# Three value buffers, reciprocals on SyncE's queue and an earlier normalization in an attention kernel with two feed-forward layers

## The chip, the core and the metric

The kernel runs on one core of a Trainium2 chip. Its engines work side by side: TensorE (PE; its weight loads are shown as PEld), VectorE (DVE), ScalarE (ACT), GpSimd (POOL) and SyncE (SP), which here does nothing but issue DMA transfers. Each engine takes its own instructions in order and waits where an operand or a buffer isn't ready. The 16 DMA engines of the core are shared by all transfers, whichever engine issued them. The metric is the time of one execution in microseconds, the median over several.

## The reference

Attention with a soft cap on its scores, then a feed-forward layer, then a gated one with a root-mean-square norm in front of it. All of it is float32.

```python
scores = scale * np.matmul(q, k.transpose(0, 1, 3, 2))     # q, k, v: (2, 12, 448, 64)
scores = cap * np.tanh(scores / cap)
attn = np.exp(scores - np.max(scores, axis=-1, keepdims=True))
attn = attn / (np.sum(attn, axis=-1, keepdims=True) + 1e-09)
x = np.matmul(attn, v)                                     # turned to (896, 768)
h = x @ w_in                                               # (768, 2048)
x = (h * (1.0 / (1.0 + np.exp(-1.702 * h)))) @ w_out       # (2048, 768)
xn = x / np.sqrt(np.mean(x * x, axis=-1, keepdims=True) + 1e-06) * rms_g
g = xn @ w_gate                                            # (768, 1536), w_val alike
out = (g * (1.0 / (1.0 + np.exp(-g))) * (xn @ w_val)) @ w_out2
```

## The kernel before

The 24 heads are taken two at a time: 12 pairs, six of each batch. A loop (in `attention`) runs over steps 0 to 12. Step p makes the scores of pair p, and in the same step finishes the pair before it. So that every product keeps nearly all float32 bits, operands are split into a rounded high part and a remainder, and three products are summed.

What one step does, engine by engine:

- **PE**: the score products of the pair in four chunks of keys (`scores`, three chunks of 128, and `scores_last`), the transposes of the pair two ahead (`turn`), the first chunk of the next pair, the weighted values of the pair before (`outputs(p - 1)`, line 360, 16 products), and the sums of its weights (`sums(p - 1)`, line 392). Outputs, sums and last chunks share two PSUM buffers (`ps_v`). So `outputs` has to wait until the buffer of the sums of one step before has been read by the reciprocal.
- **ACT**: tanh and exp of every chunk (lines 344 and 345).
- **DVE**: splits the turned q and k of the pair two ahead (lines 295 and 296), adds the first two chunks of weights (`add_two`, line 376) and for the first six pairs the third too (`add_third`, line 379), copies the outputs out of PSUM (`z`, line 368), normalizes an older pair (`normal`: lines 422, 434 and 441), and takes the reciprocal of the sums (`rs`, line 397). Where `add_third` isn't done, PE sums the third chunk by four products of its own (`v<-tt,ones`).
- **POOL**: a small copy of k (`kb`), and the two transfers that spread the reciprocals. `keep_recips` writes four rows of 224 reciprocals to DRAM (`recs<-rs`), and a step later `spread` reads them back as two rows of 448, each repeated on 64 partitions (`r<-recs`, 128 x 448 floats). The product with `r` (line 422) needs it. Pairs 9, 10 and 11 don't use this way: `spread_product` spreads their reciprocals by PE.
- **SP**: loads of q and k (`load_k`, `load_q`, eight transfers for a group of one or two pairs, into two buffers `raws`), of v (`load_v`, one transfer `vn` and two `ve`, into two buffers taken by the group's number modulo 2), and of the feed-forward weights (`load_to`, 768 KB each, `raw`). The groups are (first pair, pairs): (0,1), (1,2), (3,1), (4,2), (6,2), (8,2), (10,2).

The order on every engine is the order of the calls in this loop; no scheduler moves anything. A normalization comes four pairs late: step p calls `normal(p - 4)` behind `outputs(p - 1)`. Weight loads follow at the end of steps 1, 2 and 4, value loads at the end of steps 1, 3, 4, 6 and 8. The pair-by-pair decoding of the first weight units stands in two tables by step, `plan_a` for ACT and `plan_d` for DVE: a weight arrives as 64-bit words and is turned into a high and a low part (`size`, `clip`, `field`, `top`, `low`, `high_part`, `low_part`). `low` of a unit also issues the load of the unit three later.

Step 12 has no scores: it finishes pair 11 and goes over into `rest`, where PE multiplies by the feed-forward weights (lines 619 to 621, later 829) until the end. Its first two columns of work need the weight units 0 and 1 decoded and the first six pairs normalized; between them stands the `spread_product` of pair 11.

Of the kernel before, what the change touches and what calls it, by code (L numbers as in the profile page):

```python
# [18 lines left out]
def attn_moe_kernel(  # L19
# [174 lines left out]
    def attention():  # L194
        with ExitStack() as actx:
# [15 lines left out]
            vns = [ap_.tile([128, 4, NC, D], F32, name=f"vn{i}", bufs=1) for i in range(2)]  # L211
            ves = [ap_.tile([128, 2, 2, D], F32, name=f"ve{i}", bufs=1) for i in range(2)]
# [36 lines left out]
            def load_v(g):  # L249
# [3 lines left out]
                    out=vns[g % 2][:, 0:2 * n].rearrange("p h c d -> p h (c d)"),  # L253
                    in_=v[b, h0:h0 + 2 * n, 0:NC * 128].rearrange("h (p c) d -> p h (c d)", c=NC),
                )
                for e in range(2):
                    nc.sync.dma_start(
                        out=ves[g % 2][half[e], 0:n, e], in_=rows(v, p0, n, NC * 128, S)[:, e:2 * n:2]
                    )
# [91 lines left out]
            def outputs(p, cs=range(NC + 1)):  # L351
# [5 lines left out]
                for c in cs:  # L357
                    for e in range(2):
                        w = vns[g % 2][:, 2 * i + e, c] if c < NC else ves[g % 2][:, i, e]
# [12 lines left out]
            SH = S // 2  # L372

# [7 lines left out]
            def sums(p):  # L381

                ps = ps_v.tile([128, 512], F32, tag="v", name="v")
                for c in (1, NC) if p < NP else (1, 2, NC):
# [14 lines left out]
            def keep_recips(p):  # L399
                rs = nr[p]  # L400
                nr[p] = dram.tile([4, SH], F32, tag="recs", name="recs", bufs=3)
                nc.gpsimd.dma_start(out=nr[p], in_=rs[0:128:32])

            def spread(p):
                d = nr[p].rearrange("(e j) n -> e (j n)", j=2)
                nr[p] = zrp.tile([128, S], F32, tag="r", name="r", bufs=3)
                nc.gpsimd.dma_start(out=nr[p], in_=d.unsqueeze(1).to_broadcast([2, 64, S]))
# [58 lines left out]
            def warm_up(times):  # L466
# [6 lines left out]
                5: [(size, 0)], 7: [(size, 1)], 9: [(high_part, 0)], 11: [(high_part, 1)],  # L473
                12: [(square, 2), (sign, 2), (mask, 2), (square, 3), (sign, 3), (mask, 3)],
# [3 lines left out]
                10: [(top, 1), (low, 1), (low_part, 0)], 11: [(low_part, 1)],  # L478
# [16 lines left out]
            for p in range(NPR + 1):  # L495
                if p < NPR:
# [14 lines left out]
                    if p + 2 < NPR:  # L511
                        turn(p + 2)
                        split_kq(p + 2)
                    if 0 < p < NPR - 1:
                        s0 = scores(p + 1, 0)
# [4 lines left out]
                else:  # L520
                    decode(plan_a, p)
                if p == 0:
# [5 lines left out]
                if p >= 4:  # L528
                    normal(p - 4)
# [13 lines left out]
                if p < NP:  # L543
# [7 lines left out]
                decode(plan_d, p)  # L551

                for g, at_ in ((2, 0), (3, 0), (4, 1), (5, 3), (6, 5)):
                    if p == at_:
                        load_k(g)
                        load_q(g)
                if p in (1, 3, 4, 6, 8):
                    load_v(2 + (1, 3, 4, 6, 8).index(p))
                if p in (1, 2, 4):
                    load_to((1, 2, 4).index(p))  # L560
# [374 lines left out]
```

## Time and profile before

| What | us |
|---|---|
| Time, median of 3 runs | 610.75 (607.37 to 612.85) |
| The profiled execution | 607.63 |
| Its span, first to last instruction | 605.9 |
| PE busy in the span | 596.1 (98%) |
| DVE busy | 456.7 (75%) |
| ACT busy | 395.0 (65%) |
| POOL busy | 69.2 (11%) |

PE is called busy nearly always, but its products are pipelined and their ends are modelled, so short waits hide in that number. A wait is better read from the times at which the same piece of work starts in two steps that follow each other. Attention takes the first 106.6 us or so; there PE, ACT and DVE all have about the same amount of work in a step, and the feed-forward part behind it is PE alone.

### The profile page before, as it was taken

What the parts mean: (1) busy time and instruction counts of PE and PEld (TensorE: products, weight loads), DVE (VectorE), ACT (ScalarE), POOL (GpSimd) and SP (SyncE); (2) the same over time, 40 slices, a digit from 0 to 9 for tenths busy, and PEclk for the clock granted to TensorE, in tenths of its full rate; (3) what the DMA queues carried; (4) which work ended last, traced back from release to release, by engine and by line L of the source; (5) the groups of instructions that cost most, each with busy time, mean ns of one, the idle gap of its engine ahead of it and who ended that gap; (6) DMA issues with size and microseconds to landing.
All of it is one profiled execution on the core that took longest, in us unless ns stands there. A gap on an engine that the chain in (4) does not pass through costs nothing.

```text
span 605.9 us, 8623 instructions
## 1 busy us (share of the span) xinstructions
PE 596.1 (98%) x3405; PEld 505.9 (83%) x3405; DVE 456.7 (75%) x558; ACT 395.0 (65%) x529; POOL 69.2 (11%) x95
## 2 busy tenths in 40 slices
PE   8999999999999999999999999999999999999997
PEld 5454554889988899888888888899989999999997
DVE  3988998698774636667788899994588897688842
ACT  6998998499775547777676666674555493366400
POOL 4221321000000000000022203200022200122100
PEclk9999999999999999999999999999999999999999
DMA  6777232064343332333333333433233342232012
GB/s 152 157 194 187 67 113 84 9 203 151 111 157 104 105 105 80 123 111 105 104 105 109 100 106 107 140 117 106 62 124 116 116 134 85 96 104 105 0 79 105
DMA packets 78568, 67.18 MB, mean 111 GB/s; under 512 B 29440, under 2 KB 75830, under 8 KB 78528
## 3 DMA queue, kind: packets, MB, share of 16 engines
q1 hardware_dynamic: 74064, 64.27, 33.9%
q0 software_dynamic: 3664, 2.16, 1.3%
q8 instruction: 27, 0.44, 0.3%
q10 hardware_dynamic: 800, 0.20, 0.1%
q14 instruction: 13, 0.11, 0.1%
HBM read 63.80 MB, written 2.78 MB: 110 GB/s over the span
## 4 chain that ended last, share of the span: by engine, by line
PE 88%; DMA 7%; ACT 3%; DVE 1%; issue 1%; POOL 0%; POOLq 0%
PE b L621 22%; PE b L620 22%; PE b L619 22%; PE b L829 14%; DMA recs<-rs 4%; PE v L360 3%; PE s L322 2%; DMA ve<-in_v 1%; DMA r<-recs 1%; ACT tt L345 1%; ACT tt L344 1%; PE v L392 1%; PE v L468 1%; PE v L332 1%; PE t L274 0%
## 5 line engine op out<-in xcount | busy, mean ns | idle before, releaser
L621 PE MATMUL b<-x,ring 128*128 128x512 f32 (+1 forms) x480 | 174.3, 363 | 0.0
L620 PE MATMUL b<-x,ring 128*128 128x512 f32 (+1 forms) x480 | 174.1, 363 | 0.0
L619 PE MATMUL b<-x,ring 128*128 128x512 f32 (+1 forms) x480 | 173.9, 362 | 0.0
L619 PEld LDWEIGHTS b<-x,ring 128*128 128x128 f32 x480 | 90.1, 188 | 10.4 <-issue 0.3
L620 PEld LDWEIGHTS b<-x,ring 128*128 128x128 f32 x480 | 90.1, 188 | 9.9
L621 PEld LDWEIGHTS b<-x,ring 128*128 128x128 f32 x480 | 90.1, 188 | 9.4
L829 PE MATMUL b<-ring,uA 128*128 128x384 f32 x504 | 87.8, 334 | 0.0
L829 PEld LDWEIGHTS b<-ring,uA 128*128 128x128 f32 x504 | 87.4, 188 | 0.0
L154 DVE SCALAR_TENSOR_TENSOR dec<-raw,dec 128x768 uint32<-128x768 uint32 x66 | 67.8, 1027 | 24.7 <-ACT dec L150 23.4
L160 DVE SCALAR_TENSOR_TENSOR dec<-raw,dec 128x768 uint32<-128x768 uint32 x68 | 73.1, 1075 | 1.1
L175 ACT ACTIVATE ring<-dec 128x768 fp32r<-128x768 f32 x68 | 56.7, 834 | 21.9 <-DVE dec L166 13.7
L180 DVE TENSOR_TENSOR ring<-dec,ring 128x768 fp32r<-128x768 f32 x68 | 66.8, 983 | 4.5 <-ACT ring L175 4.5
L621 PE MATMUL b<-g,ring 128*128 128x384 f32 (+1 forms) x192 | 70.0, 365 | 0.0
L620 PE MATMUL b<-g,ring 128*128 128x384 f32 (+1 forms) x192 | 69.9, 364 | 0.0
L619 PE MATMUL b<-g,ring 128*128 128x384 f32 (+1 forms) x192 | 69.6, 362 | 0.0
L166 DVE SCALAR_TENSOR_TENSOR dec<-raw,dec 128x768 uint32<-128x768 uint32 x68 | 64.9, 954 | 1.5
L146 ACT ACTIVATE dec<-dec,edge 128x768 f32<-128x768 f32 x66 | 61.5, 932 | 1.0
L142 ACT ACTIVATE dec<-raw 128x768 f32<-128x768 f32 x66 | 59.2, 897 | 0.5 <-DVE ring L180 0.5
L150 ACT ACTIVATE dec<-dec 128x768 f32<-128x768 f32 x66 | 55.6, 843 | 1.5
L797 POOL TENSOR_TENSOR a<-a,gg 128x512 f32<-128x512 f32 (+1 forms) x18 | 29.6, 1646 | 188.6 <-DVE gg L790 188.6
L800 ACT ACTIVATE uA<-a 128x512 fp32r<-128x512 f32 (+1 forms) x24 | 13.9, 578 | 46.3 <-POOL a L797 34.5
L651 DVE TENSOR_TENSOR g<-gg,g 128x384 fp32r<-128x384 f32 (+1 forms) x32 | 20.0, 625 | 25.9 <-ACT g L648 25.7
(107 smaller groups left out, 680.2 us busy)
## 6 DMA issues: line engine op xcount, KB each, us to landing
raw<-in_moe_w_out SPq DMA_DIRECT2D x20, 768.0 KB, 4.2
raw<-in_moe_w_in SPq DMA_DIRECT2D x16, 768.0 KB, 4.5
raw<-in_moe_w_gate SPq DMA_DIRECT2D x12, 768.0 KB, 4.2
raw<-in_moe_w_val SPq DMA_DIRECT2D x12, 768.0 KB, 4.2
raw<-in_moe_w_out SPq DMA_DIRECT2D x8, 512.0 KB, 3.6
out<-oacc SPq DMA_DIRECT2D x6, 384.0 KB, 2.3
raw<-in_moe_w_out SPq DMA_DIRECT2D x8, 256.0 KB, 3.1
r<-recs POOLq DMA_DIRECT2D x9, 224.0 KB, 7.4
```

Source lines behind the costliest of these rows:

```text
L142: nc.scalar.activation(out=f(d), in_=f(hi), func=AF.Square, scale=2.0 ** 15)
L146: nc.scalar.activation(out=f(d), in_=f(d), func=AF.Sign, bias=edge)
L150: nc.scalar.activation(out=f(d), in_=f(d), func=AF.Relu, scale=2.0 - 2.0 ** -23)
L154: nc.vector.scalar_tensor_tensor(out=d, in0=hi, scalar=3, in1=d, op0=ALU.logical_shift_left, op1=ALU.bitwise_and)
L160: nc.vector.scalar_tensor_tensor(out=d, in0=hi, scalar=0xC0000000, in1=d, op0=ALU.bitwise_and, op1=ALU.bitwise_or)
L166: nc.vector.scalar_tensor_tensor(out=d, in0=lo, scalar=29, in1=d, op0=ALU.logical_shift_right, op1=ALU.bitwise_or)
L175: nc.scalar.activation(out=t[:, 0], in_=f(dec_t[w][0]), func=AF.Copy)
L180: nc.vector.tensor_tensor(out=t[:, 1], in0=f(d), in1=f(t[:, 0]), op=ALU.subtract)
L619: nc.tensor.matmul(out=wide(o, b), lhsT=w0, rhs=x0, start=first, stop=False)
L620: nc.tensor.matmul(out=wide(o, b), lhsT=w0, rhs=x1, start=False, stop=False)
L621: nc.tensor.matmul(out=wide(o, b), lhsT=w1, rhs=x0, start=False, stop=last)
L829: nc.tensor.matmul(out=os_[t][n][:, 0:HW], lhsT=uA[xi][:, i, tok], rhs=w[:, wi, n * HW:(n + 1) * HW], start=(i == 0 and xi == 0 and wi == ...
```

## The change

Five things are changed, all in `attention`:

1. The value buffers `vns` and `ves` are three each, taken by the group's number modulo 3.
2. `keep_recips` and `spread` issue their transfers on SP's queue, not on POOL's.
3. `normal` is called for pair p - 3 in steps 3 to 11 (before: pair p - 4 in steps 4 to 12). The calls for the pairs 9 and 10 stay where they were.
4. `add_third` is also done for pairs 10 and 11, and `sums` leaves the third chunk out for them.
5. `high_part` of units 0 and 1 is done in steps 10 and 12 (before 9 and 11), `low_part` in steps 11 and 12 (before 10 and 11), ahead of the sums of pair 11 in step 12. The loads of q, k, v and weights are called in the middle of a step, ahead of `spread` and `keep_recips`. Values are loaded in steps 1, 2, 4, 5 and 7, and the first three weight units in steps 2, 4 and 6.

```diff
-            vns = [ap_.tile([128, 4, NC, D], F32, name=f"vn{i}", bufs=1) for i in range(2)]
-            ves = [ap_.tile([128, 2, 2, D], F32, name=f"ve{i}", bufs=1) for i in range(2)]
+            vns = [ap_.tile([128, 4, NC, D], F32, name=f"vn{i}", bufs=1) for i in range(3)]
+            ves = [ap_.tile([128, 2, 2, D], F32, name=f"ve{i}", bufs=1) for i in range(3)]
...
+            THIRD = {*range(NP), NPR - 2, NPR - 1}
...
-                for c in (1, NC) if p < NP else (1, 2, NC):
+                for c in (1, NC) if p in THIRD else (1, 2, NC):
...
-                nc.gpsimd.dma_start(out=nr[p], in_=rs[0:128:32])
+                nc.sync.dma_start(out=nr[p], in_=rs[0:128:32])
...
-                nc.gpsimd.dma_start(out=nr[p], in_=d.unsqueeze(1).to_broadcast([2, 64, S]))
+                nc.sync.dma_start(out=nr[p], in_=d.unsqueeze(1).to_broadcast([2, 64, S]))
...
+                    for g, at_ in ((2, 0), (3, 0), (4, 1), (5, 3), (6, 5)):
+                        if p == at_:
+                            load_k(g)
+                            load_q(g)
+                    if p in (1, 2, 4, 5, 7):
+                        load_v(2 + (1, 2, 4, 5, 7).index(p))
+                    if p in (2, 4, 6):
+                        load_to((2, 4, 6).index(p))
                     if 0 < p < NPR - 1:
                         s0 = scores(p + 1, 0)
...
                 else:
                     decode(plan_a, p)
+                    decode(plan_d, p)
...
-                if p >= 4:
-                    normal(p - 4)
+                if 3 <= p < NPR:
+                    normal(p - 3)
...
-                if p < NP:
+                if p in THIRD:
                     add_third(p)
...
-                decode(plan_d, p)
-
-                for g, at_ in ((2, 0), (3, 0), (4, 1), (5, 3), (6, 5)):
...
-                if p in (1, 3, 4, 6, 8):
-                    load_v(2 + (1, 3, 4, 6, 8).index(p))
-                if p in (1, 2, 4):
-                    load_to((1, 2, 4).index(p))
+                if p < NPR:
+                    decode(plan_d, p)
```

On SP's queue, behind the value load of step 1, the order was this (two lines of the kernel move to other numbers with the change: 402 becomes 403, 407 becomes 408):

```order
L252 DMA vn_104<-in_v 128x2x192
L257 DMA ve_106<-in_v 64x64 x2
L113 DMA raw<-in_moe_w_in 128x6x256 x2
L237 DMA kq_103<-in_k 64x4x64
L239 DMA kq_103<-in_k 128x4x64 x3
L245 DMA kq_103<-in_q 64x4x64
L245 DMA kq_103<-in_q 128x4x64 x3
L252 DMA vn_105<-in_v 128x4x192
L257 DMA ve_107<-in_v 64x2x64 x2
```

And with the change, from the reciprocals that step 1 keeps on to those that step 3 keeps:

```order
L403 DMA recs<-rs 4x224
L252 DMA vn_104<-in_v 128x4x192
L257 DMA ve_107<-in_v 64x2x64 x2
L113 DMA raw<-in_moe_w_in 128x6x256
L408 DMA r<-recs 128x1x448
L403 DMA recs<-rs 4x224
L237 DMA kq_103<-in_k 64x4x64
L239 DMA kq_103<-in_k 128x4x64 x3
L245 DMA kq_103<-in_q 64x4x64
L245 DMA kq_103<-in_q 128x4x64 x3
L408 DMA r<-recs 128x1x448
L403 DMA recs<-rs 4x224
```

The value load that stood behind a weight pair and eight loads of q and k now stands ahead of them, and each `r` stands behind all loads of its step.

On DVE, from the reciprocal of pair 9's sums (step 10) into step 12, before:

```order
L397 RECIPROCAL rs<-v 128x224
L160 SCALAR_TENSOR_TENSOR dec<-raw,dec 128x768
L166 SCALAR_TENSOR_TENSOR dec<-raw,dec 128x768
L180 TENSOR_TENSOR ring<-dec,ring 128x768
L376 TENSOR_TENSOR ts<-tt 128x896
L368 COPY z<-v 128x448
```

and with the change:

```order
L398 RECIPROCAL rs<-v 128x224
L380 TENSOR_TENSOR ts<-ts,tt 128x896
L160 SCALAR_TENSOR_TENSOR dec<-raw,dec 128x768
L166 SCALAR_TENSOR_TENSOR dec<-raw,dec 128x768
L377 TENSOR_TENSOR ts<-tt 128x896
L368 COPY z<-v 128x448
```

The addition of the third chunk came in, and the low part of unit 0 (line 180) went out, to a place behind the normalizations of step 11, where both low parts now stand in a row ahead of the last reciprocal:

```order
L398 RECIPROCAL rs<-v 128x224
L380 TENSOR_TENSOR ts<-ts,tt 128x896
L426 TENSOR_TENSOR z<-z,late 128x448
L435 CAST x_66<-z 128x448
L442 TENSOR_TENSOR x_67<-z,x_66 128x448
L180 TENSOR_TENSOR ring<-dec,ring 128x768 x2
L398 RECIPROCAL rs<-v 128x224
```

Before, a whole normalization (lines 422, 434 and 441) stood between the low part of unit 1 and that last reciprocal; it is now done in step 11.

## Rows read from the trace of the kernel before

**Rows 1.** Busy time of the two stages; stretch, length, then each engine's busy us:

```profile
0.00:106.60 106.60, 101.03 (x873) 52.82 (x873) 87.26 (x107) 94.88 (x110) 27.94 (x67) 1.00 0.52 136
106.60:605.90 499.30, 495.07 (x2536) 453.06 (x2532) 369.48 (x451) 300.16 (x420) 41.29 (x28) 1.00 0.32 106
```

**Rows 2.** TensorE in order of time, outputs of pairs 3 to 6 (start us, us):

```profile
41.00 2.48 PE L360 MATMUL v<-tt,vn 128*64 128x448 f32 x12
...
44.16 0.59 PE L392 MATMUL v<-ts,ones 128*32 128x224 f32 x8
...
48.52 2.48 PE L360 MATMUL v<-tt,vn 128*64 128x448 f32 x12
...
52.64 0.97 PE L360 MATMUL v<-tl,ve 128*64 128x448 f32 x2 [0.90 <-DMA ve<-in_v]
...
57.90 2.48 PE L360 MATMUL v<-tt,vn 128*64 128x448 f32 x12
...
65.42 2.48 PE L360 MATMUL v<-tt,vn 128*64 128x448 f32 x12
```

**Rows 3.** VectorE in order of time, steps 3, 6 and 10:

```profile
36.78 0.63 DVE L368 COPY z<-v 128x448 f32<-128x448 f32 x1 [0.57 <-PE v L360]
37.67 1.56 DVE L397 RECIPROCAL rs<-v 128x224 f32<-128x224 f32 x1 [0.26 <-PE v L392]
...
61.94 0.61 DVE L422 TENSOR_TENSOR z<-z,r 128x448 f32<-128x448 f32 x1
...
63.56 1.55 DVE L397 RECIPROCAL rs<-v 128x224 f32<-128x224 f32 x1
...
92.41 0.62 DVE L368 COPY z<-v 128x448 f32<-128x448 f32 x1 [1.93 <-PE v L360]
```

**Rows 4.** GpSimd in order of time, the issue of one `r`:

```profile
69.17 0.80 POOL L407 DMA_DIRECT2D r<-recs  x1 [5.02 <-DMA recs<-rs]
```

**Rows 5.** Line 407, and the nearest load by SP: issue to landing, us:

```profile
DMA to landing us min/median/max: 6.8/7.4/11.9
...
vn<-in_v SPq DMA_DIRECT2D x2, 192.0 KB, 2.8
```

**Rows 6.** DMA in four stretches; the last two numbers are share of 16 engines and GB/s:

```profile
31.50:34.50 3.00, 3.00 (x30) 1.82 (x31) 2.59 (x4) 2.97 (x4) 0.57 (x1) 1.00 1.05 367
58.50:59.50 1.00, 1.00 (x8) 0.34 (x6) 0.96 (x2) 1.00 (x2) 0.00 (x0) 1.00 0.83 205
62.00:62.50 0.50, 0.50 (x9) 0.47 (x8) 0.50 (x2) 0.50 (x1) 0.50 (x2) 1.00 1.01 318
95.00:99.00 4.00, 3.69 (x21) 1.52 (x19) 3.97 (x5) 2.57 (x4) 0.00 (x0) 1.00 0.13 49
```

**Rows 7.** SyncE's issues in order of time, steps 1 and 2:

```profile
27.41 1.13 SPq L257 DMA_DIRECT2D ve<-in_v  x2
28.59 1.18 SPq L113 DMA_DIRECT2D raw<-in_moe_w_in  x2
```

**Rows 8.** VectorE and TensorE where attention ends, in order of time:

```profile
104.90 0.95 DVE L180 TENSOR_TENSOR ring<-dec,ring 128x768 fp32r<-128x768 f32 x1
107.45 0.63 DVE L422 TENSOR_TENSOR z<-z,r 128x448 f32<-128x448 f32 x1 [1.60 <-DMA r<-recs]
...
109.09 1.55 DVE L397 RECIPROCAL rs<-v 128x224 f32<-128x224 f32 x1
...
106.63 0.44 PE L619 MATMUL b<-x,ring 128*128 128x384 f32 x1
...
109.68 0.34 PE L621 MATMUL b<-x,ring 128*128 128x384 f32 x1
...
111.33 0.44 PE L619 MATMUL b<-x,ring 128*128 128x384 f32 x1
```

**Rows 9.** Third chunk, groups by line (busy us, mean ns): added on DVE, summed on PE:

```profile
L379 DVE TENSOR_TENSOR ts<-ts,tt 128x896 f32<-128x896 f32 x6 | 6.3, 1048 | 0.1
...
L392 PE MATMUL v<-tt,ones 128*32 128x224 f32 x48 | 3.4, 353 | 0.0
```

More of the change, by code (lines that the diff above doesn't have):

```diff
@@ L252, in load_v @@
                 nc.sync.dma_start(
-                    out=vns[g % 2][:, 0:2 * n].rearrange("p h c d -> p h (c d)"),
+                    out=vns[g % 3][:, 0:2 * n].rearrange("p h c d -> p h (c d)"),
                     in_=v[b, h0:h0 + 2 * n, 0:NC * 128].rearrange("h (p c) d -> p h (c d)", c=NC),
@@ L257, in load_v @@
                     nc.sync.dma_start(
-                        out=ves[g % 2][half[e], 0:n, e], in_=rows(v, p0, n, NC * 128, S)[:, e:2 * n:2]
+                        out=ves[g % 3][half[e], 0:n, e], in_=rows(v, p0, n, NC * 128, S)[:, e:2 * n:2]
                     )
@@ L358, in outputs @@
                     for e in range(2):
-                        w = vns[g % 2][:, 2 * i + e, c] if c < NC else ves[g % 2][:, i, e]
+                        w = vns[g % 3][:, 2 * i + e, c] if c < NC else ves[g % 3][:, i, e]
                         nc.tensor.matmul(
@@ L472, in attention @@
             plan_a = {
-                5: [(size, 0)], 7: [(size, 1)], 9: [(high_part, 0)], 11: [(high_part, 1)],
-                12: [(square, 2), (sign, 2), (mask, 2), (square, 3), (sign, 3), (mask, 3)],
+                5: [(size, 0)], 7: [(size, 1)], 10: [(high_part, 0)],
+                12: [(high_part, 1), (square, 2), (sign, 2), (mask, 2), (square, 3), (sign, 3), (mask, 3)],
             }
@@ L477, in attention @@
                 6: [(clip, 0), (field, 0)], 7: [(top, 0)], 8: [(low, 0)], 9: [(clip, 1), (field, 1)],
-                10: [(top, 1), (low, 1), (low_part, 0)], 11: [(low_part, 1)],
+                10: [(top, 1), (low, 1)], 11: [(low_part, 0)], 12: [(low_part, 1)],
             }
@@ L550, in attention @@
                     normal(p - 2)
-                decode(plan_d, p)
-                for g, at_ in ((2, 0), (3, 0), (4, 1), (5, 3), (6, 5)):
-                    if p == at_:
-                        load_k(g)
-                        load_q(g)
-                if p in (1, 3, 4, 6, 8):
-                    load_v(2 + (1, 3, 4, 6, 8).index(p))
-                if p in (1, 2, 4):
-                    load_to((1, 2, 4).index(p))
+                if p < NPR:
+                    decode(plan_d, p)
             return spread_product, norm_mul, norm_hi, norm_lo
```

## Prediction

> **What bounds the kernel now.** I read the stages first. From 106.6 us on PE is busy for 495.07 of 499.30 us [rows 1]; the change touches nothing there, so that part can only start earlier or later. All that can be won or lost lies ahead of 106.6 us. There PE is busy for 101.03 and DVE for 87.26 of 106.60 us, so neither is idle for long, and what a single wait is worth must be read from times of start.
>
> On PE the outputs of one pair start 7.52 us after those of the pair before (41.00 to 48.52), but the next start 9.38 later (48.52 to 57.90): in between stands a wait for `ve`, shown as 0.90 us, and the difference of 1.86 us is its price [rows 2]. On DVE a step from one normalization to its reciprocal takes 1.62 us (61.94 to 63.56) and a reciprocal 1.56 [rows 3]. Behind attention's end a last `r` is late: DVE waits for it for 1.60 us and then normalizes until 109.09, ahead of the last reciprocal, for which PE's second column of feed-forward work waits; that column starts at 111.33, 4.70 us after the first [rows 8].
>
> Then the transfers of the reciprocals. `r` takes 6.8 us at the least from issue to landing, where an SP load of nearly its size (192 KB) takes 2.8 [rows 5]. The reason stands in a stretch in which `r` alone is in flight: 0.13 of 16 engines are busy, that is two, and they move 49 GB/s [rows 6]. The 224 KB (229 kB) of one `r` take 229/49 = 4.7 us, and 2.1 us lie around that. I put 1.5 of them ahead of the data and 0.6 behind, which is an estimate. Two engines fit the source, which is two rows, each repeated for 64 partitions.
>
> **What each part costs.**
>
> *Third value buffer, values loaded sooner.* The load that came late goes to SP at about 29 us (behind the value load of step 1, 28.54 below) and is needed behind 48.52. This gives back the 1.86 us on PE [rows 2]. Weight units are loaded up to two steps later and are decoded from step 5 on, the last of the three only in step 12, so that costs nothing; were a unit not there, ACT would stop at its first decoding.
>
> *Reciprocals through SP.* The pattern of `r` isn't changed, only the queue. No row shows such a pattern on SP's queue. Its bounds are the 2.8 us of the SP load and the 6.8 us of `r` itself [rows 5]; I take 6.8, 4.7 of it on two engines, since the two rows of the source are what makes the difference and they stay. The Trainium skill, "DMA: Bandwidth & Descriptors", section "Why a DMA increments its semaphore by 16 and not by 1", says that the number of engines is the largest up to 16 that divides the slowest dimension of both sides, for transfers from POOL and from SP alike. The trace agrees for POOL's queue (0.13 of 16 [rows 6]), and no run here shows it for SP's. By that rule it is two here as well, and the sum is the one below; were it POOL's alone, it would be that of the first rival.
>
> What the queue does change is the order. SP's transfers go through these two engines one behind the other, and each `r` now stands behind the loads of its step. Their time on the engines comes from full-rate stretches [rows 6]: a weight unit (786 kB at 367 GB/s) 2.1 us, a group's q and k (918 kB at 205) 4.5, a group's values (459 kB at 318) 1.4. SP now also waits for each step's reciprocal before it goes on to the next step's loads; these are needed two steps later or more, so that wait costs nothing by itself. POOL loses its waits for `recs` (5.02 us in one step [rows 4]), but only the small `kb` copies stand behind them and nobody waits for those.
>
> *Normalization a pair sooner.* `r` of pair p - 3 is needed in step p, one step earlier than before. What is late then is DVE: behind its wait stand the reciprocal of the step, and behind that PE's next outputs, which need the reciprocal's PSUM buffer. So I follow `r` from pair to pair. With every `r`, normalization (1.62), reciprocal (1.56) and outputs follow; the next `r` is due 3.16 us of outputs (41.00 to 44.16 [rows 2]) and 0.68 for the hand-over and the copy (0.63 [rows 3]) later, 3.84 in all.
>
> - r(0): SP is through with the value load of step 1 at 28.54 (27.41 + 1.13 [rows 7]). Then come `recs`, three value transfers and a weight unit, 0.6 us an issue [rows 7], so `r` is issued at 31.6. The weight unit, issued at 31.0, has its data on the engines from 32.5 to 34.6. r(0) lands at 34.6 + 4.7 + 0.6 = 39.9. It is due behind the copy at 36.78, at 37.3 [rows 3]: 2.6 late. Reciprocal until 43.1, outputs of pair 3 at 43.1 and not 41.00.
> - r(1) stands behind eight loads of q and k: 39.3 + 4.5 + 4.7 + 0.6 = 49.1. Due at 43.1 + 3.84 = 46.9: 2.2 late. Outputs of pair 4 at 52.3.
> - r(2) stands behind values and a weight unit: 48.5 + 1.4 + 2.1 + 4.7 + 0.6 = 57.3. Due at 56.1: 1.2 late. Outputs of pair 5 at 60.5.
> - r(3) stands behind q, k and values: 56.7 + 4.5 + 1.4 + 4.7 + 0.6 = 67.9. Due at 64.3: 3.6 late. Outputs of pair 6 at 71.1, where they were at 65.42 [rows 2]: 5.7 us later.
> - r(4) stands behind a weight unit: 67.3 + 2.1 + 4.7 + 0.6 = 74.7. Due at 74.9: in time. Behind it come one value group and two weight units in six steps, and no further `r` is late.
>
> The 1.86 us of the removed wait are in this already, since each pair is set by its `r`.
>
> *Third chunk and decoding at the end.* With steps as before, the copy of pair 9's outputs moves by 5.7 from 92.41 [rows 3] to 98.1. From there DVE is never idle in the trace until the low part of unit 1 at 104.90 [rows 8], 12.5 us. The same instructions now end with unit 0's low part, and two additions of the third chunk come in, 1.05 us each with about 0.1 overlapped [rows 9], 1.9 in all: 98.1 + 12.5 + 1.9 = 112.5. PE needs this low part 0.3 us into its first column, so the column starts at 112.2, 5.6 later than 106.63 [rows 8]. PE itself would be there at 106.63 + 5.7 less two third-chunk sums (3.4/6 = 0.57 at most each [rows 9]), about 111.2; so the saving on PE is lost to DVE. What is saved is behind that. The wait of 1.60 and the normalization of 1.64 (107.45 to 109.09 [rows 8]) are no longer there; the low part of unit 1 (0.95) and the reciprocal (1.55) end at 115.0, before PE is through its first column at 115.4 (from 106.63 to the last product's start at 109.68 and that product, 3.2 us [rows 8]). With 0.5 us of `spread_product` (of the 0.69 from the reciprocal's end, 109.09 + 1.55, to 111.33) the second column starts at 115.9, and not at 111.33: +4.6 us.
>
> **The sum.** Span 605.9 + 4.6 = 610.5, and the profiled execution of 607.63 becomes 612.2. That execution is 3.1 us below the median of the runs (610.75), so for a median I add to the median: 610.75 + 4.6 = **615.4 us**, 0.8% more. A measurement of this kernel can tell about 1% from no change, some 6.1 us, and this is less.
>
> **The rivals.**
>
> *`r` is quick on SP's queue.* For it speaks the 2.8 us of the SP load [rows 5], against it the two rows of the source. Then r(0) lands at about 36.5 and no normalization waits. The wait for `ve` is gone: the copy of pair 9 moves by -1.86 to 90.55, DVE has unit 0 at 90.55 + 12.5 + 1.9 = 104.95, the first column starts at 104.65 and the second 3.7 us later at 108.35, which is 3.0 less than 111.33. Time: 607.8 us. A gain over 1% isn't in it, since all that is there to win is the `ve` wait and the end. The Trainium skill, same page, section "Issuing engines are not separate DMA queues", says that another issuing engine saves only its own issue time; by that `r` would not become quicker on SP's queue, and no run here shows it.
>
> *SP's queue stands still behind each `r`.* If SP cannot issue the next loads while the two engines are full of an `r`, these loads start only when it has drained, and the 1.5 us ahead of the data are paid anew on idle engines: behind r(0) to r(3), four times, 6.0 us, on top of the 4.6. Time: 621.4 us. For it speaks that nothing lets a transfer pass another on this queue; against it that two 768 KB weight units were issued in 1.18 us, one behind the other, with no halt [rows 7]. Two of the four (7.6 us in all) are enough for slower by over 1%.
>
> *The transfer's pieces are smaller than I take them.* Each late `r` is a difference of sums of about 10 us; at a full DMA share of 1.00 instead of 0.83 a group of q and k takes 3.7 us, not 4.5 [rows 6], and r(3) is then earlier by 1.6 us (two groups): +3.0, 613.8 us. It belongs to the forecast's own range.
>
> **How the numbers follow.** Late `r` as worked out, with its own range from 613 to 617: 0.62. Quick `r`: 0.20. SP stands still: 0.15. Something unforeseen: 0.03. The range must leave out no more than 0.2: it reaches down to the quick case with 1 us to spare (606.7) and up to two and a half of the four halts (619). Slower by over 1%: the 0.15, and 0.04 from the forecast's upper end. Faster by over 1%: 0.03, if the quick case wins more at the end than I see. The same: 0.78.
>
> **What would show it.** Right: DVE waits for `r` at its normalization in steps 3 to 6, for about 2.6, 2.2, 1.2 and 3.6 us, and not later; `r` takes 7 to 11 us to land in these steps and 6 to 7 afterwards; a stretch with `r` alone shows two engines, near 49 GB/s; PE has no wait for `ve`; the first column starts near 112, bound by the low part of unit 0, and the second 3.7 us later. Wrong: `r` lands within 3 us on SP's queue, or DVE waits for it in no step; then the gain of some 3 us is there. Wrong the other way: SP issues with gaps of several us behind each `r`, and DVE waits beyond step 7.

## The result and the profile after

| | before | after |
|---|---|---|
| median of 6 runs each, us | 608.94 | 616.25 |
| ratio, 95% interval | | 1.0114 [1.0079, 1.0148] |
| profiled execution, us | 607.63 | 615.20 |
| its span, us | 605.9 | 613.4 |
| normalizations waiting for `r` (us in all) | 1, at the end (1.60) | 4, steps 3 to 6 (7.8) |
| first, second column of feed-forward work starts, us | 106.63, 111.33 | 114.02, 118.73 |

The changed kernel is slower by 1.1%. The forecast was 615.4 us, 0.8% more, with "within 1%" as the likeliest of the three; the ratio lies just beyond that line, with its interval on both sides. The shift of the second column (7.40 us) is the whole change of the span (7.5): the stages after, cut where the feed-forward work starts, answer to [rows 1], and the second is as long as it was, 499.4 us against 499.30. (Columns: stretch, length, busy us of PE, PEld, DVE, ACT and POOL, granted clock, DMA share, GB/s.)

```profile
0.00:114.00 114.00, 101.58 (x857) 53.20 (x857) 89.00 (x111) 93.05 (x107) 18.64 (x51) 0.99 0.48 127
114.00:613.40 499.40, 495.51 (x2536) 453.23 (x2532) 369.69 (x451) 302.53 (x422) 41.30 (x28) 1.00 0.33 106
```

TensorE in order of time, outputs of pairs 3 to 6 (start us, us, then the instruction, and in brackets its idle time and what ended it). They stand where [rows 2] has 41.00, 48.52, 57.90 and 65.42:

```profile
43.08 2.48 PE L360 MATMUL v<-tt,vn 128*64 128x448 f32 x12 [1.33 <-DVE rs L398]
...
52.85 2.48 PE L360 MATMUL v<-tt,vn 128*64 128x448 f32 x12 [2.18 <-DVE rs L398]
...
61.45 2.48 PE L360 MATMUL v<-tt,vn 128*64 128x448 f32 x12 [1.01 <-DVE rs L398]
...
72.45 3.86 PE L360 MATMUL v<-tt,vn 128*64 128x448 f32 x12 [3.42 <-DVE rs L398]
```

PE waits for DVE's reciprocal each time, and DVE has waited for `r` (the multiplication of line 423, steps 3 to 6; all of its waits for `r`):

```profile
39.84 0.63 DVE L423 TENSOR_TENSOR z<-z,r 128x448 f32<-128x448 f32 x1 [1.76 <-DMA r<-recs]
...
49.61 0.63 DVE L423 TENSOR_TENSOR z<-z,r 128x448 f32<-128x448 f32 x1 [1.99 <-DMA r<-recs]
...
58.21 0.63 DVE L423 TENSOR_TENSOR z<-z,r 128x448 f32<-128x448 f32 x1 [0.82 <-DMA r<-recs]
...
69.22 0.62 DVE L423 TENSOR_TENSOR z<-z,r 128x448 f32<-128x448 f32 x1 [3.23 <-DMA r<-recs]
```

A stretch with one `r` alone in flight, now through SP's queue, shows the same two engines as [rows 6] (share 0.13, 49 GB/s):

```profile
70.80:72.00 1.20, 0.00 (x0) 0.00 (x0) 1.20 (x2) 1.17 (x3) 0.00 (x0) 0.94 0.13 49
```

SyncE's issues show a wait that the prediction doesn't have. `recs` of one pair stands right behind `r` of the pair before it, and the next `r` is issued only at 49.83, where r(1) has just landed (DVE goes on at 49.61):

```profile
41.73 0.55 SPq L408 DMA_DIRECT2D r<-recs  x1
43.05 0.55 SPq L403 DMA_DIRECT2D recs<-rs  x1
...
49.83 0.56 SPq L408 DMA_DIRECT2D r<-recs  x1
```

Of SyncE's waits between 25 and 75 us this is the largest (us in all, times, longest):

```profile
SPq L408 <- DMA recs<-rs: 9.8, 2, 6.2
```

And TensorE's granted clock (the number ahead of the last two) was at 0.50, its 1.2 GHz level, while the outputs of pair 6 ran; before and behind it was at 2.4 GHz:

```profile
70.00:71.00 1.00, 0.00 (x0) 0.00 (x0) 0.97 (x3) 0.97 (x2) 0.00 (x0) 1.00 0.11 41
...
73.00:74.00 1.00, 1.00 (x4) 0.24 (x2) 1.00 (x2) 0.97 (x2) 0.00 (x0) 0.50 0.13 45
...
76.00:77.00 1.00, 1.00 (x8) 0.15 (x4) 0.53 (x1) 0.00 (x0) 0.94 (x2) 1.00 0.34 91
```

At the end of attention, DVE's low parts of both units in one row, the last reciprocal, and PE's two columns; they answer to [rows 8]:

```profile
113.98 1.82 DVE L180 TENSOR_TENSOR ring<-dec,ring 128x768 fp32r<-128x768 f32 x2
115.72 1.55 DVE L398 RECIPROCAL rs<-v 128x224 f32<-128x224 f32 x1
```

```profile
114.02 0.44 PE L621 MATMUL b<-x,ring 128*128 128x384 f32 x1
...
114.98 0.44 PE L623 MATMUL b<-x,ring 128*128 128x384 f32 x1 [0.34 <-DVE ring L180]
...
117.71 0.34 PE L623 MATMUL b<-x,ring 128*128 128x384 f32 x1
117.98 0.82 PE L414 MATMUL b<-rs,sel 32*64 32x224 f32 x8
118.73 0.45 PE L621 MATMUL b<-x,ring 128*128 128x384 f32 x1
```

### The profile page after: what moved, and what is told of

It reads as the page before. It is cut to its first block, busy times and chain, and to the rows that moved or that the text cites. A ratio compares the mean times of both kernels' runs of the same rounds, so it can differ in the third digit from the quotient of the medians.

```text
span 613.4 us, 8590 instructions
## 1 busy us (share of the span) xinstructions
PE 597.1 (97%) x3389; PEld 506.4 (83%) x3389; DVE 458.7 (75%) x560; ACT 395.6 (64%) x529; POOL 59.9 (10%) x79
## 4 chain that ended last, share of the span: by engine, by line
PE 90%; DVE 3%; ACT 3%; DMA 3%; issue 1%; SPq 0%
PE b L623 22%; PE b L622 22%; PE b L621 22%; PE b L831 14%; PE v L360 4%; DMA r<-recs 3%; PE s L322 2%; PE v L393 1%; ACT tt L345 1%; ACT tt L344 1%; DVE rs L398 1%; PE v L332 1%; PE v L469 1%; PE t L274 0%; DVE ts L380 0%
## 5 line engine op out<-in xcount | busy, mean ns | idle before, releaser
L802 ACT ACTIVATE uA<-a 128x512 fp32r<-128x512 f32 (+1 forms) x24 | 13.9, 579 | 46.3 <-POOL a L799 34.5
L344 ACT ACTIVATE tt<-s,tsc 128x896 f32<-128x896 f32 x36 | 35.8, 994 | 11.4 <-PE s L322 11.4
```

## The experiments

All ratios are to the kernel before, run beside. Medians in us; the waits are DVE's waits for `r` from 25 to 125 us, in the one profiled execution of each kernel. Three further kernels (e8_loads_pool, e7_busy, e7b_busy) are told of in their places.

| kernel | queue of recs, r | normalized | pieces of r | waits for `r` | span | median | ratio, 95% interval |
|---|---|---|---|---|---|---|---|
| after | SP, SP | p - 3 | 1 | 7.8 (4) | 613.4 | 616.25 | 1.0114 [1.0079, 1.0148] |
| e1_pool | POOL, POOL | p - 3 | 1 | 6.3 (4) | 611.2 | 614.89 | 1.0098 [1.0062, 1.0133] |
| e2_late | SP, SP | p - 4 | 1 | 3.0 (1) | 608.0 | 609.56 | 1.0010 [0.9989, 1.0031] |
| e6_recs_pool | POOL, SP | p - 3 | 1 | 5.1 (3) | 611.7 | 614.08 | 1.0076 [1.0048, 1.0105] |
| e3_halves | SP, SP | p - 3 | 2 | 1.8 (1) | 605.1 | 606.38 | 0.9967 [0.9946, 0.9988] |
| e5_nothird | SP, SP | p - 3 | 2 | 0.3 (1) | 602.8 | 605.90 | 0.9945 [0.9918, 0.9972] |
| e12_pool_halves | POOL, POOL | p - 3 | 2 | 0 | 602.2 | 605.34 | 0.9941 [0.9918, 0.9963] |
| e10_oldplan | SP, SP | p - 3 | 2 | 0.3 (1) | 604.2 | 606.53 | 0.9959 [0.9938, 0.9979] |
| e9_values | POOL, POOL | p - 4 | 1 | 3.9 (3) | 606.8 | 608.34 | 0.9996 [0.9968, 1.0025] |
| e11_values_halves | POOL, POOL | p - 4 | 2 | 0 | 603.9 | 605.17 | 0.9941 [0.9920, 0.9962] |

**Queue or place.** e1_pool undoes the queue alone:

```diff
-                nc.sync.dma_start(out=nr[p], in_=rs[0:128:32])
+                nc.gpsimd.dma_start(out=nr[p], in_=rs[0:128:32])
...
-                nc.sync.dma_start(out=nr[p], in_=d.unsqueeze(1).to_broadcast([2, 64, S]))
+                nc.gpsimd.dma_start(out=nr[p], in_=d.unsqueeze(1).to_broadcast([2, 64, S]))
```

> The changed kernel with one part undone: the reciprocals' two transfers (keep_recips, spread) go through GpSimd's queue again; all else stays. Theory A (an r takes 4.7 us on two engines, and due a pair sooner it is late on either queue; the order behind the loads adds some of it): the chain recs to r on that queue was 7.3 to 8 us a step before, and r is now due one step sooner, so DVE still waits for r in steps 3 and later, by 1 to 4 us each, and the time stays between 612 and 620 us. Theory B (SP's queue alone is to blame, the sooner normalization costs nothing): no waits for r, the gain of the removed ve wait is left, about 606 to 608 us, that is 0.98 to 1.00 of the kernel before.

It is slow in the same way, 1.0098, with waits of 1.87, 1.59, 1.09 and 1.71 us in steps 3 to 6. Theory B, SP's queue alone, falls. GpSimd's issues show the chain there: each `r` waits for its `recs`, and the issues lie 9.3 and 8.9 us apart, more than a step of 7.5 [rows 2].

```profile
39.65 0.97 POOL L408 DMA_DIRECT2D r<-recs  x1 [3.01 <-DMA recs<-rs]
42.66 0.57 POOL L403 DMA_DIRECT2D recs<-rs  x1 [2.03 <-DVE rs L398]
...
48.99 1.00 POOL L408 DMA_DIRECT2D r<-recs  x1 [2.06 <-DMA recs<-rs]
...
57.87 0.99 POOL L408 DMA_DIRECT2D r<-recs  x1 [1.56 <-DMA recs<-rs]
```

With DVE's rows one round of this chain can be followed. r(0) has come at 39.18; behind that normalization stands the reciprocal of pair 2, whose `recs` is issued at 42.66 and lets r(2) be issued at 48.99; r(2) has come at 57.43, 18.25 us after r(0).

```profile
39.18 0.62 DVE L423 TENSOR_TENSOR z<-z,r 128x448 f32<-128x448 f32 x1 [1.87 <-DMA r<-recs]
...
40.81 1.55 DVE L398 RECIPROCAL rs<-v 128x224 f32<-128x224 f32 x1
...
57.43 0.63 DVE L423 TENSOR_TENSOR z<-z,r 128x448 f32<-128x448 f32 x1 [1.09 <-DMA r<-recs]
```

At p - 3 this round has two steps, 15.0 us at 7.5 each, so `r` falls behind (in the kernel after it takes 18.37 us, from 39.84 to 58.21). At p - 4 the normalization of pair 0 stands ahead of the reciprocal of pair 3 instead, and the same round would have three steps, 22.5 us. That is why one step decides, on either queue.

e2_late undoes the place alone:

```diff
-                if 3 <= p < NPR:
-                    normal(p - 3)
+                if p >= 4:
+                    normal(p - 4)
```

> The changed kernel with one part undone: normalization stands a pair later again (normal(p - 4) from step 4 on); the reciprocals still go through SP's queue. Theory A (late r because it is due a step sooner, behind loads and on two engines): each r has 8 to 9 us more, DVE waits for none of them in steps 4 to 8, the removed ve wait is kept as a gain of 1.9 us, the TensorE clock has no dip between 60 and 80 us, and the time is about 607 us (605 to 609), 0.99 to 1.00 of the kernel before. Theory C (the end, with the third chunk and decoding moved, is to blame and not r): the time stays above 612 us.

Three of the four waits are gone; r(3) still comes 2.97 us late, the clock is again 0.83 between 70 and 80 us (theory A had neither), and the gain of the `ve` wait is spent on that: 609.56 us, 1.0010, just above theory A's 605 to 609 and under theory C's 612. So most of the loss comes from asking for `r` a step sooner, and SP's queue has a share of its own, r(3). Its rows show where: seven loads of q and k take 8.54 us to issue (4.05 from 22.67 us on in the kernel before, where no `r` is in flight yet), so r(3) is issued at 63.22, 11.8 us behind its `recs`.

```profile
70.90 0.62 DVE L423 TENSOR_TENSOR z<-z,r 128x448 f32<-128x448 f32 x1 [2.97 <-DMA r<-recs]
```

```profile
51.37 0.55 SPq L403 DMA_DIRECT2D recs<-rs  x1
...
52.69 3.40 SPq L239 DMA_DIRECT2D kq<-in_k  x3
56.19 5.14 SPq L245 DMA_DIRECT2D kq<-in_q  x4
...
63.22 0.55 SPq L408 DMA_DIRECT2D r<-recs  x1
```

**The two engines.** e3_halves changes how `r` is cut and nothing else:

```diff
-                nc.sync.dma_start(out=nr[p], in_=d.unsqueeze(1).to_broadcast([2, 64, S]))
+                for e in range(2):
+                    nc.sync.dma_start(out=nr[p][half[e]], in_=d[e:e + 1].to_broadcast([64, S]))
```

> The changed kernel with one size changed: spread() issues two transfers of 64 partitions, each from one row of the source, instead of one of 128 partitions from two rows. Theory A (two rows of the source put each r on two engines, 4.7 us): each half is now free to be spread over all 16 engines, r lands about 3 to 4 us after its issue, DVE waits for r in no step, or for under 1 us in all; the ve gain stays, and with the clock undisturbed the first column starts near 105 and the second near 108.5: about 605.5 us (604 to 608), that is 0.99 to 1.00 of the kernel before and 10 us under the changed kernel. Theory D (what makes r late is only its place behind the loads, or repetition of one row as such): the waits of 1.8, 2.0, 0.8 and 3.2 us stay within 1 us each, and the time is 613 to 617 us.

0.9967: one edit of `r`'s shape takes back the whole loss and some more. Theory D falls. Where the halves are alone in flight the share is 0.78 and not 0.13, SP's waits for `recs` (25 to 110 us) fall from 16.5 us to 3.5 (that sum is no price by itself: e2_late has 33.3 and is faster than the kernel after), and a half lands in 4.4 us (median; a whole `r` on GpSimd's queue took 7.4 [rows 5]). The round from r(0) to r(2), 18.25 us in e1_pool, is now about 11 (39.14 to the issue at 45.72, and 4.4 until a half lands), under the 15.0 of two steps. What is left is r(0), 1.77 us late behind a weight unit, more than the 1 us expected; in e5_nothird, which is the same kernel up to step 10, it is 0.3, so single executions differ there.

```profile
76.50:77.00 0.50, 0.50 (x14) 0.38 (x16) 0.50 (x2) 0.47 (x1) 0.50 (x1) 1.00 0.78 229
```

```profile
SPq L409 <- DMA recs<-rs: 3.5, 4, 1.1
```

```profile
r<-recs SPq DMA_DIRECT2D x18, 112.0 KB, 4.4
```

e12_pool_halves puts `recs` and both halves on GpSimd's queue instead (with the third chunk undone as in e5_nothird, below):

```diff
-                    nc.sync.dma_start(out=nr[p][half[e]], in_=d[e:e + 1].to_broadcast([64, S]))
+                    nc.gpsimd.dma_start(out=nr[p][half[e]], in_=d[e:e + 1].to_broadcast([64, S]))
```

> The kernel with r in halves and without the third chunk for the last two pairs, but recs and both halves of r on GpSimd's queue. Theory E (what counts is on how many engines r lies; the queue is worth little): no wait for r beyond 1 us in all, and 605 to 607 us, within 0.2% of the same kernel on SP's queue. Theory B (SP's queue is the gain in itself, since GpSimd's takes 6 us or more for any such transfer): DVE waits for r in steps 3 to 6 again, by 1 us each or more, and the time is 608 us or more.

0.9941 against 0.9945, with no wait for `r`; a half lands there in 2.9 us. The queue is worth nothing that can be told once `r` lies on more engines.

```profile
r<-recs POOLq DMA_DIRECT2D x18, 112.0 KB, 2.9
```

**The chain from r to recs to r.** e6_recs_pool moves `recs` alone off SP's queue (the first two lines of e1_pool's diff).

> The changed kernel with only the small transfer recs (keep_recips) back on GpSimd's queue; r stays on SP's. In the changed kernel SP stands at r until recs has landed, and recs stands in SP's queue right behind the r of the pair before, so each r can be issued only when the one before it has landed (r(2) is issued at 49.83, where r(1) lands at about 49.6). Theory E (this chain from r to recs to r sets the late r from the second on): recs lands 2 to 3 us after its reciprocal, r(2) is issued near 46.3 and no normalization of step 5 waits; the waits of steps 4 to 6 fall from 6.0 us together to under 4, and the time to 611 to 614 us. Theory A as predicted (loads ahead on the same two engines set it, recs' place is nothing): the waits stay within 0.5 us each, and the time is 614.5 to 617 us.

Nearer to theory E than to A, though within neither: r(2) is issued at 47.53 and not 49.83 (46.3 was expected), step 5 waits no more, the waits of steps 4 to 6 fall from 6.0 us to 4.4 (under 4 was expected), and the ratio falls from 1.0114 to 1.0076 (the intervals overlap). But `recs`, 3.5 KB on a queue of its own, still takes 4.6 us to land, twice what I expected, and r(3) is again issued behind the slow q and k loads (59.71, with its `recs` kept at 51.69): 2.73 us late. As long as `r` lies on two engines, both steps of the chain are slow. The clock hides a part of the gain: it falls twice here, and the outputs of pairs 4 and 6 take 4.11 and 3.62 us instead of 2.48, 2.77 us more together, where the kernel after loses 1.38.

```profile
recs<-rs POOLq DMA_DIRECT2D x9, 3.5 KB, 4.6
```

e8_loads_pool takes the loads away from `r`'s queue instead (five times the same edit):

```diff
-                nc.sync.dma_start(out=t[0:64, NC, 0:2 * n], in_=rows(k, p0, n, NC * 128, S))
+                (nc.sync if g < 2 else nc.gpsimd).dma_start(out=t[0:64, NC, 0:2 * n], in_=rows(k, p0, n, NC * 128, S))
```

> The changed kernel with the loads of q, k and values from the third group on issued on GpSimd's queue, so that r and recs share SP's queue with the weight units alone. Theory A (each r stands behind its step's loads in one queue): the waits for r in steps 4 and 6, whose r stands behind q and k, fall from 2.0 and 3.2 us to under 1 us each; the time is 609 to 612 us. Theory E (the chain from r to recs to r of about 8 us a step sets it, whatever else is on the queue): r still lands every 8 us or more from r(0) on, the waits of steps 3 to 6 stay at 5 us or more together, and the time is 613 to 617 us.

As a timing it failed: 622.23 us, 1.0209 [1.0177, 1.0241], since a new delay came in: outputs of pair 2 start at 40.31, where they are at 34.11 in e6_recs_pool. PE stands still for 4.6 us in all (from 18.6 to 25.4 us) for the q and k of pair 3, which GpSimd issues from 18.35 us on, behind a `kb` copy, where SyncE issues them from 11.37 in the kernel after. Of its waits for `r` it says what theory E expects, if not of the time: without q, k and values on SP's queue they are still 6.6 us together (0.71, 3.12 and 2.77), and those of steps 4 and 6 are not under 1 us, as theory A has them. The loads of q, k and values ahead in the queue are not by themselves what makes `r` late (they still share the 16 DMA engines with it).

```profile
21.34 0.28 PE L274 MATMUL t<-ident,kq 64*128 64x64 f32 x2 [2.78 <-DMA kq<-in_k]
```

```profile
DVE z L423 <- DMA r<-recs: 6.6, 3, 3.1
```

**The value buffers alone.** e9_values is the kernel before with three value buffers and the sooner loads:

```diff
-            vns = [ap_.tile([128, 4, NC, D], F32, name=f"vn{i}", bufs=1) for i in range(2)]
+            vns = [ap_.tile([128, 4, NC, D], F32, name=f"vn{i}", bufs=1) for i in range(3)]
...
-                if p in (1, 3, 4, 6, 8):
-                    load_v(2 + (1, 3, 4, 6, 8).index(p))
+                if p in (1, 2, 4, 5, 7):
+                    load_v(2 + (1, 2, 4, 5, 7).index(p))
```

> The kernel before with one part of the change alone: three value buffers, and the values loaded in steps 1, 2, 4, 5 and 7. Theory A: the wait for ve at 52.64 us is gone, and what comes behind it starts 1.86 us sooner; the end is set by the same waits as before, so the time is 606.2 us (605.5 to 607), 0.996 to 0.998 of the kernel before. Rival (the value load takes up the engines that the late r needs on the other queue, and the r of step 8 or the last one is later): no gain, 607.5 to 609 us.

0.9996: the rival's time, though by a different way. The `ve` wait is gone and outputs of pair 6 start at 63.51 (65.42 before [rows 2]), 1.91 sooner, but the last three `r` are now late, and the gain is given back there:

```profile
92.10 0.63 DVE L422 TENSOR_TENSOR z<-z,r 128x448 f32<-128x448 f32 x1 [0.67 <-DMA r<-recs]
...
100.89 0.62 DVE L422 TENSOR_TENSOR z<-z,r 128x448 f32<-128x448 f32 x1 [1.40 <-DMA r<-recs]
...
108.37 0.62 DVE L422 TENSOR_TENSOR z<-z,r 128x448 f32<-128x448 f32 x1 [1.87 <-DMA r<-recs]
```

So the kernel before stood at the limit of this chain already: without the `ve` wait its `r` can't follow. e11_values_halves adds the two halves to e9_values (e3_halves' edit on GpSimd's queue):

> The kernel before with three value buffers (values in steps 1, 2, 4, 5, 7) and, in addition, r in two halves; queue, place of the normalization and end as before. Theory E (three value buffers alone gained nothing, since the chain r to recs to r on two engines could not follow the quicker steps): with r in halves over more engines no normalization waits for r, the 1.86 us of the ve wait are kept to the end and the last wait of 1.60 us is gone: 605 to 606.5 us, about 0.995 of the kernel before. Rival (something else took the gain): the first column stays at about 105.9 and the second at 111, and the time within 0.2% of the kernel before.

0.9941, no wait for `r`: with the chain loosened, the value buffers and the removed last wait pay what they should. Nothing else of the change is in this kernel, and it is as fast as e5_nothird and e12_pool_halves (0.9945 and 0.9941): with `r` in halves, the queue, the sooner normalization and the later decoding together show no gain in the time.

**The end.** e5_nothird is e3_halves with the third chunk for the last two pairs undone, and e10_oldplan is e5_nothird with the decoding where it was before:

```diff
-            THIRD = {*range(NP), NPR - 2, NPR - 1}
+            THIRD = {*range(NP)}
```

> The kernel with r in two halves, and the third chunk's additions for the last two pairs taken out again (PE sums three chunks there, as before). With r in time, DVE is what sets the end: two additions of 1.05 us each with 0.1 overlapped are 1.9 us of DVE against 0.57 us of PE for each pair. Expected: unit 0's low part ends up to 1.9 us earlier, PE comes to its first column up to 1.1 us later; the time is that of the kernel with two halves or up to 1 us less (604 to 606 us). If PE sets the end there, it is up to 1.1 us more.

```diff
-                5: [(size, 0)], 7: [(size, 1)], 10: [(high_part, 0)],
-                12: [(high_part, 1), (square, 2), ...
+                5: [(size, 0)], 7: [(size, 1)], 9: [(high_part, 0)], 11: [(high_part, 1)],
+                12: [(square, 2), ...
...
-                10: [(top, 1), (low, 1)], 11: [(low_part, 0)], 12: [(low_part, 1)],
+                10: [(top, 1), (low, 1), (low_part, 0)], 11: [(low_part, 1)],
```

> The kernel with r in halves and without the third chunk for the last two pairs, and also the plan of decoding as before (high and low part of unit 0 in steps 9 and 10, of unit 1 in 11): of the changed kernel's end nothing is left. Theory H (with r in time PE is never waited for at the end, and the decoding can stand in either place): the time is that of the same kernel with the later plan, 605 to 606.5 us. Rival (the low part of unit 0 in step 10 stands ahead of outputs that PE needs, as it did): PE's last outputs and the last reciprocal come 0.9 to 1.9 us later, 606.5 to 608 us.

The medians (606.38, 605.90, 606.53) are too close to tell apart; the profiles can. From the outputs of pair 10 to the second column it takes 14.60 us in the kernel after and in e3_halves, and 13.80 in e5_nothird and e12_pool_halves: the third chunk for two pairs costs 0.8 us here, since DVE is late with the additions and the low parts and PE waits for both (0.65 and 0.34 us in e3_halves). In e10_oldplan it takes 14.31, and from pair 8 to pair 9 it takes 8.07 us where e12_pool_halves has 7.47: 0.5 and 0.6, so the later decoding is worth 1.1 us in these profiles. Theory H does not hold in them; PE's waits there, between 25 and 125 us, are these (us, times, longest), where e5_nothird has one of 0.3 us for ACT and none for the copy:

```profile
PE v L393 <- ACT tl L344: 0.8, 2, 0.5
PE v L393 <- DVE z L368: 0.4, 1, 0.4
```

**The clock.** e7_busy and e7b_busy give TensorE products that nobody reads, ahead of the outputs of steps 3 to 6:

```diff
                 elif p > 2:
+                    for _ in range({3: 5, 4: 8, 5: 4, 6: 13}.get(p, 0)):
+                        nc.tensor.matmul(out=s0[:, 0, 448:512], lhsT=ident, rhs=ident[:, 0:64], start=True, stop=True)
                     outputs(p - 1)
```

> The changed kernel with idle work for TensorE where it waits: 12, 20, 9 and 32 products of 64 columns into unused columns of the score bank, ahead of the outputs in steps 3 to 6, that nobody reads. They add no wait if they are no longer than the waits there (1.33, 2.18, 1.01 and 3.42 us). Theory F (TensorE's granted clock fell between 70 and 80 us because it had stood still in the waits before): PE is busy through these waits, the granted clock stays 1.00 from 60 to 80 us, the outputs of pair 6 take 2.5 us and not 3.86, and the time is 1.4 us less than the changed kernel's, about 614.5 to 615 us. Theory G (the clock falls there for another reason): the clock shows 0.83 between 70 and 80 us again, and the time is that of the changed kernel or up to 1 us more.

> The changed kernel with idle products for TensorE in its waits, now of the right length: in the run before each took 0.24 us (2.89 us for 12), so 5, 8, 4 and 13 are 1.2, 1.9, 1.0 and 3.1 us against waits of 1.33, 2.18, 1.01 and 3.42. Nobody reads them. Theory F (the granted clock fell because TensorE had stood still in these waits): clock 1.00 from 60 to 80 us, outputs of pair 6 in 2.5 us and not 3.86, and 1.4 us less than the changed kernel beside the same start: 1.008 to 1.010 of the kernel before. Theory G (another reason): the clock falls to 0.83 between 70 and 80 us again, and the ratio stays at 1.011 or above.

The first was made with 12, 20, 9 and 32 products of 0.24 us each, twice as long as I had thought, and took 622.00 us, 1.0205 [1.0178, 1.0233]. The second took 616.09 us, 1.0123 [1.0085, 1.0161], no gain on the kernel after. I had put the products one step early: outputs of pair p - 1 stand in step p, so they lie ahead of pairs 2 to 5 and the waits were ahead of 3 to 6. They delay pair 2 and pair 5 by themselves. The clock nevertheless answers: it is 1.00 from 60 to 80 us in both, and in e7b_busy pair 6's outputs take 2.48 us, right behind a wait of 2.29. That fits theory F and does not prove it: the kernel after stayed at 1.00 behind a wait of 2.18, e6_recs_pool fell behind one of 1.80, and e2_late fell in a wait of 2.73 us that was PE's first for a reciprocal. The gain of 1.4 us that theory F had was not shown; by the time alone theory G would stand.

```profile
60.00:70.00 10.00, 10.00 (x92) 6.68 (x92) 6.83 (x8) 6.71 (x8) 1.29 (x2) 1.00 0.67 176
70.00:80.00 10.00, 7.71 (x75) 3.98 (x74) 8.86 (x13) 7.67 (x10) 1.28 (x2) 1.00 0.28 84
```

```profile
74.17 2.48 PE L360 MATMUL v<-tt,vn 128*64 128x448 f32 x12 [2.29 <-DVE rs L398]
```

## Why the prediction was right, and where it was not

- **Late `r` on two engines: right, shown.** The two engines on SP's queue (0.13, 49 GB/s) and the halves of e3_halves are the proof. By the Trainium skill, "DMA: Bandwidth & Descriptors", section "Why a DMA increments its semaphore by 16 and not by 1", the slowest dimension decides on the number of engines; the rows agree for SP's queue too, where a source of two rows took two engines and 64 partitions from one row a share of 0.78.
- **Places and sizes of the waits: right to within a microsecond.** Forecast 2.6, 2.2, 1.2 and 3.6 late, none later; DVE waited 1.76, 1.99, 0.82 and 3.23, none later. Pairs 3 to 6 were forecast at 43.1, 52.3, 60.5 and 71.1, and came at 43.08, 52.85, 61.45 and 72.45. From its issue each of these `r` took 7.8 to 8.6 us until DVE went on, where 7 to 11 was forecast.
- **The reason for them: right only in part.** The step "*SP's transfers go through these two engines one behind the other, and each `r` now stands behind the loads of its step*" carried the sum. e1_pool has no such loads in its queue and lost nearly as much; e8_loads_pool has none of q, k and values there and waits for 6.6 us. What the sum lacked is the round: the reciprocal that `recs` carries stands on DVE behind a normalization that waits for an `r`, `recs` lands only when the `r` ahead of it has, and the next `r` waits for it, on either queue: 18.25 us in e1_pool, for two steps of 7.5. With that the cause is the two engines together with the place one step sooner; the order on SP's queue adds r(3). That r(1) to r(3) came within 1.3 us of the sum all the same is in part luck: r(2) stood until 49.83 for its `recs`, and r(1) and r(3) stood behind seven loads of q and k that took 7.5 and 5.3 us to issue, not 4.2 (0.6 each).
- **"*that wait costs nothing by itself*": wrong.** SP stood at `recs` until the reciprocal of step 4 was there (52.82, with r(2) issued at 49.83), and the loads of q and k started 3.6 us behind r(2), with r(3) behind them; in e6_recs_pool they start 1.3 us behind it (48.81, with r(2) at 47.53). SP's wait for `recs` to land is not in the sum at all. e6_recs_pool, which takes `recs` with both waits off SP's queue, has 2.7 us less of late `r` and 1.7 us less of span; which of the two waits gives how much, it does not say.
- **The rival "SP's queue stands still": SP does issue slowly, but it did so before, with `r` on the other queue.** Four issues of q took 5.29 us behind r(0) and 3.59 behind r(2), where the prediction has 0.6 each.

```profile
36.38 5.29 SPq L245 DMA_DIRECT2D kq<-in_q  x4
...
55.94 3.59 SPq L245 DMA_DIRECT2D kq<-in_q  x4
```

The kernel before has the same, with `r` on GpSimd's queue: 2.35 us for four while no `r` is in flight, and 3.95 beside r(0), with three issues of k ahead of them that took 5.26. So the slow issues are not new; the change puts r(1) and r(3) behind them. They were not four halts of 1.5 us on top of the sum.

```profile
24.46 2.35 SPq L245 DMA_DIRECT2D kq<-in_q  x4
...
33.40 5.26 SPq L239 DMA_DIRECT2D kq<-in_k  x3
38.76 3.95 SPq L245 DMA_DIRECT2D kq<-in_q  x4
```

- **The rival "`r` is quick": not true of SP's queue, but its price was near.** It was put at 3.0 us under the kernel before; the change with `r` in halves is 2.0 us under it (e3_halves, 0.9967 of 608 us). The 3.6 us of 0.9941 are reached only by kernels that leave out other parts of the change too.
- **The 1.86 us of the `ve` wait: the place was right, the worth was not.** Alone they are worth nothing (e9_values), because `r` is the next limit; with halves they come through (e11_values_halves).
- **The end: right in kind.** The first column was held up by the low part of unit 0 (the wait of 0.34 us), as forecast. From pair 6, the clock's loss included, to the second column 1.01 us were won back, where the forecast had 1.1. But e11_values_halves, with the end of the kernel before, has lost its last wait for `r` too and is as fast as any, so the new end is worth little in itself, which fits the terms found: -1.1 for the later decoding, +0.8 for the third chunk.
- **The size: 4.6 forecast, 7.40 measured at the second column.** Pair 6 came 7.03 later and not 5.7, 1.33 more: r(0) came when it was forecast (39.84, forecast 39.9), but r(1), r(2) and r(3) at 49.61, 58.21 and 69.22, where the sum had 49.1, 57.3 and 67.9. (The copy of step 3 stands at 37.46 in this execution, 0.68 later than in [rows 3], but DVE waited for r(0) behind it all the same.) The clock, not foreseen, added 1.38 (3.86 less 2.48). Up to the first column 1.03 was regained, where the forecast had 0.1. And the second column came 4.71 behind the first, not 3.7: the wait of 0.34 stretched the first, 0.2 is the sum's own ([rows 8] give 3.39 us for a column, 106.63 to 109.68 and 0.34, where it has 3.2), and from the last `spread_product` to the column it took 0.75 instead of 0.5. The sum: 4.6 + 1.33 + 1.38 - 0.93 + 1.01 = 7.39. That the median came within 1 us of the forecast is in part luck: the time moved by 7.3 us and not 4.6, but from 608.94 over six runs and not from 610.75.

Still open: why `recs` takes 4.6 us on a queue of its own, why issues of q and k are slow beside an `r` on two engines, and which wait of PE is followed by the lower clock. The new places of the loads in a step were not undone alone.

## What to carry to other kernels

Read the share of the DMA engines where a transfer is alone in flight: 0.13 says that its shape, and not its queue, sets its time, and cutting the source so that each piece has many rows of its own is worth more than moving it. Where a small transfer and a large one alternate in a loop and each waits for the other, add up the time round the loop and hold it against as many steps as the loop spans, before a consumer is moved forward and takes one step off it. And a wait that is removed pays only as far as the next chain that runs at nearly the same pace: the best kernels here, 0.994 of the time before, have `r` in two halves, and one of them nothing else but the third value buffers with their sooner loads.

## What the runs showed of the hardware

- TensorE's granted clock fell from its 2.4 GHz to its 1.2 GHz level (0.50 at 72 to 75 us) in a wait of 3.42 us, and in other runs in or behind waits of 1.90 (e1_pool), 2.73 (e2_late), 1.80 and 2.48 us (e6_recs_pool); outputs of 2.48 us then took 3.6 to 4.1. Behind 2.18 us in the kernel after, 2.29 in e7b_busy and 2.35 in e9_values it did not fall, so the last wait's length alone does not decide. No kernel with `r` in halves showed it in these stretches.
- A transfer of 3.5 KB took 2.8 us (median) to land on GpSimd's queue where `r` lay in halves (e12_pool_halves), and 4.6 on the same queue where `r` lay on two engines through SP's (e6_recs_pool). By the Trainium skill, "DMA: Bandwidth & Descriptors", section "Issuing engines are not separate DMA queues", transfers of all issuing engines share the same DMA engines; the two times agree with it.
- Four issues of q on SyncE took 2.35 us in the kernel before as long as no `r` was in flight (from 24.46). Beside an `r` on two engines they took 3.2 to 7.3 us, whether `r` was on GpSimd's queue (3.95 and 4.47 in the kernel before, 7.32 in e9_values) or on SP's (5.14 in e2_late); beside an `r` in halves 2.4 to 3.2 (2.44 in e3_halves, 3.17 in e11_values_halves).
